# Causal attention and a max-of-three feed-forward on one core: eleven places for raw weights, low bits on GpSimd, one ring for outputs and maxima, a new plan

## The chip, the cores and the metric

The kernel runs on one core of one Trainium2 chip. A core has five instruction streams that run side by side and meet only at semaphores: TensorE (PE: matmuls, with its weight loads shown as PEld), VectorE (DVE), ScalarE (ACT), GpSimd (POOL) and SyncE (SP), which here only starts transfers. Each stream runs in the order in which it was written: an instruction that waits holds up all behind it on its engine. Matmuls write to PSUM, a small memory of banks, and DVE and ACT copy the results from there to SBUF, the core's working memory.

The metric is the device time of one launch in microseconds (us). The profile splits the same time into what each engine did.

## The reference

```python
scores = scale * np.matmul(q, k.transpose(0, 1, 3, 2))          # batch 8, heads 8, seq 576, dim 64
cum = np.cumsum(np.maximum(s, 0.0), axis=-1)
bias = -(cum[:, :, :, None] - cum[:, :, None, :])
scores = np.where(causal, -1000000000.0, scores + np.minimum(bias, 0.0))
scores = scores - np.max(scores, axis=-1, keepdims=True)
attn = np.exp(scores)
attn = attn / (np.sum(attn, axis=-1, keepdims=True) + 1e-09)
out = np.matmul(attn, v)
...
x = np.ascontiguousarray(out.transpose(0, 2, 1, 3)).reshape(B * S, H * D)   # 4608 x 512
h = np.maximum(np.maximum(x @ w1, x @ w2), x @ w3)                          # w1, w2, w3: 512 x 768
return h @ w_out                                                            # w_out: 768 x 512
```

Sixty-four heads of causal attention with a bias that decays with the distance, and then a feed-forward ("experts") whose hidden layer is the largest of three projections. All is fp32 outside.

## The kernel before

**Work.** The projections are made from pairs of 16-bit numbers: x, the weights and h are each split into a high half in fp16 and a low half that holds the rest, and each product is three fp16 matmuls (high by high, high by low, low by high). A token set is one batch in one of two phases: phase 0 has its first 256 queries, phase 1 the other 320. So there are sixteen expert sets. A set has 18 up groups (`u`, six tiles of the hidden layer by three weights, 12 matmuls each, L1479) and four down groups (`d`, 18 matmuls each, L1535).

**A set's steps.** Of three up groups of a tile the first is copied from PSUM to a buffer `m` (ACT L1490 or DVE L1494); the other two are taken into it by a scaled maximum (DVE L1502). ACT makes the high half of `h` (L1509), POOL the low one (L1514). A finished down group is scaled into an output buffer `o` by ACT (L1554) and sent by SP (L1560, `out_dram<-o`). `m` has three buffers in turn, `o` two. PSUM has three banks for `u`, `d` and whatever else goes by the name `m`.

**Set 0 is plain.** Batch 0, phase 0 is projected in fp32 straight from the raw weights (L659 to L677, down L689) while these are still being split. A raw weight is 128 x 512 numbers of 64 bits; 24 of them are loaded by SP (L477). Each goes from 64 bits to 32 by ACT (`d1`, L485), by DVE, and, from the third on, by POOL for its lowest bits (L499; the constant LOWP says which). Then a small gram product on PE (L527), its largest sum and a power of two (DVE L425 and L442, PE L434, together "power") give the scale of four weights at once; ACT makes the high half of `w` (L599), DVE the low half (L637). Raw weights lie in six places r0 to r5 and a few early buffers; each place is used again when all readers of its last weight are done.

**Attention.** It runs in units: "split" (256 queries of two head pairs of a batch), "rest" (the other 320 of one pair) and "whole" (all 576 of one pair). ORDER names them by batch: `s0` is the split units of batch 0, `r0` its rest, `w7` batch 7 whole. A unit loads q, k (`qr`) and v (`rv`) through SP, splits them (L949, L961), or for the first RAWS split units scores them in fp32 as they come. Its bias comes from running sums that DVE scans once for all heads (L375): SP spreads them to all rows from a copy in DRAM (`cd`, L880), for units 0 and 1 PE broadcasts them instead (L918). POOL lays in the causal mask (L1222). Then come the scores on PE (L1149), and the unit adds the bias and takes the row maximum on DVE (L1235), exponentials on ACT (L1244), 1/sum (L1252, L1262), splits the probabilities into two halves (ACT L1280, DVE L1288), transposes them through SP's DMAs (L1299), multiplies by v (L1384) and splits the result into x (L1429 and on).

**What sets the order.** Nothing is scheduled by the compiler: a planner in the kernel (class `Plan`) simulates the five engines. Each operation is added with the engines that may do it, a pair of durations, a key and what it reads and writes. At each moment `run` gives each free engine the ready operation with the smallest key, provided the buffers that it opens are free in the simulation; `write` then emits all in that order. For a transfer the planner keeps one clock per queue. A tag's buffers are a ring: of the kind "order" they are used in the order of creation, of the kind "free" in the order in which operations start. Constants such as PACE, EARLY, LOOK, HOLD and LATE shift keys: how far experts run behind attention, how early loads go out, how long PE keeps one tiling mode. So a constant moves instructions on every engine.

## Time and profile before

| | us |
|---|---|
| median of three timed runs | 784.83 |
| lowest and highest of the three | 783.97, 786.31 |
| the profiled execution's own time | 784.61 |
| its span in the profile | 782.6 |

| engine | busy, us | share of the span | instructions |
|---|---|---|---|
| PE | 764.8 | 98% | 7189 |
| DVE | 573.8 | 73% | 1691 |
| ACT | 519.2 | 66% | 1369 |
| POOL | 308.3 | 39% | 361 |

The profile page gives busy time by engine, the span in 40 slices (each digit the busy tenths of a slice), the DMA queues, the chain of work that ended last, and groups of instructions. A group's row reads: line, engine, operation, out<-in by the program's names, partitions x elements, count | busy us, mean ns of one | idle time of the engine just before them, and what ended most of it. The costliest groups:

```profile
L1479 PE MATMUL u<-x,w 128*128 128x320 f16 (+1 forms) x3240 | 411.3, 287 | 2.9 <-ACT o L1554 2.9
L1535 PE MATMUL d<-h,w 128*128 128x320 f16 (+1 forms) x1080 | 137.9, 287 | 0.1
L1502 DVE SCALAR_TENSOR_TENSOR m<-u,m 128x320 f32<-128x320 f32 (+1 forms) x180 | 82.2, 457 | 64.3 <-PE u L1479 60.1
```

The mean of the first row, 287 ns, is that of one form only and the row mixes two; 3240 up matmuls take 411.3 us together, and 1080 down matmuls 137.9.

A row of the timeline reads: start in us, length, engine, line, operation, tiles, count, and in brackets how long the engine had waited and for whom. A window's row reads: stretch, length, then the busy time of PE, PEld, DVE, ACT and POOL (with counts), the granted clock of PE, the share of DMA busy and GB/s.

### The profile page before, as it was taken

How to read it: one execution, taken by the hardware profiler on the slowest of the kernel's cores; microseconds unless marked ns; L12 is line 12 of the kernel's file. 1: busy time of each engine (PE TensorE's matmuls, PEld its weight loads, DVE VectorE, ACT ScalarE, POOL GpSimd, SP SyncE). 2: the span in 40 equal slices, each digit the busy share in tenths (PEclk: the TensorE clock that was granted, in tenths of full speed). 3: DMA queues.
4: the chain of work that ended last, by engine and by line, in shares of the span. 5: the costliest groups of instructions: out<-in, count | busy, mean ns of one | idle time of the engine just before them, and what ended most of it. 6: DMA issues, size and time to landing. Idle time of an engine off the chain costs nothing. (4 is left out here: it accounts for less than half of the span.)

```text
span 782.6 us, 19630 instructions
## 1 busy us (share of the span) xinstructions
PE 764.8 (98%) x7189; PEld 589.6 (75%) x7189; DVE 573.8 (73%) x1691; ACT 519.2 (66%) x1369; POOL 308.3 (39%) x361
## 2 busy tenths in 40 slices
PE   7889999999999999999999899999999999999998
PEld 5677888888888877766788677667776777778875
DVE  6999898875587888888878787888787977322131
ACT  6878777871687787986887777777876977111101
POOL 4432423641355455444544364354444452011110
PEclk9999999999999999999999999999999999999999
DMA  9799778890399899998999999898989865300000
GB/s 342 245 260 242 180 169 164 176 237 18 97 207 233 199 175 214 227 215 200 225 232 207 183 192 240 241 190 198 254 210 169 208 137 100 81 1 34 28 2 34
DMA packets 241167, 136.31 MB, mean 174 GB/s; under 512 B 204080, under 2 KB 222000, under 8 KB 241072
## 3 DMA queue, kind: packets, MB, share of 16 engines
q1 hardware_dynamic: 240912, 134.78, 75.7%
q8 instruction: 56, 0.92, 0.5%
q14 instruction: 39, 0.32, 0.2%
q10 hardware_dynamic: 160, 0.30, 0.1%
HBM read 75.64 MB, written 9.58 MB: 109 GB/s over the span
## 5 line engine op out<-in xcount | busy, mean ns | idle before, releaser
L1479 PE MATMUL u<-x,w 128*128 128x320 f16 (+1 forms) x3240 | 411.3, 287 | 2.9 <-ACT o L1554 2.9
L1479 PEld LDWEIGHTS <-w 128*128 128x128 f16 x3240 | 312.6, 98 | 99.5 <-issue 17.6
L1514 POOL TENSOR_TENSOR h<-m,h 128x320 f16<-128x320 f32 (+1 forms) x90 | 69.9, 777 | 190.4 <-ACT h L1509 174.5
L1535 PE MATMUL d<-h,w 128*128 128x320 f16 (+1 forms) x1080 | 137.9, 287 | 0.1
L1502 DVE SCALAR_TENSOR_TENSOR m<-u,m 128x320 f32<-128x320 f32 (+1 forms) x180 | 82.2, 457 | 64.3 <-PE u L1479 60.1
L1535 PEld LDWEIGHTS <-w 128*128 128x128 f16 x1080 | 104.7, 98 | 30.4 <-issue 3.2
L1222 POOL TENSOR_SCALAR_AFFINE_SELECT p<-bias 128x256 f32<-128x256 f32 (+3 forms) x91 | 68.9, 770 | 120.6 <-DVE pr L1288 68.9
L1244 ACT ACTIVATE p<-p,sc 128x256 f32<-128x256 f32 (+3 forms) x182 | 98.2, 540 | 26.3 <-DVE sc L1235 25.6
L1509 ACT ACTIVATE h<-m 128x320 f16<-128x320 f32 (+1 forms) x90 | 39.4, 438 | 102.9 <-DVE m L1502 102.6
L1288 DVE SCALAR_TENSOR_TENSOR pr<-p,sc,pr 128x256 f16<-128x256 f32 (+3 forms) x182 | 100.3, 567 | 8.0 <-ACT pr L1280 7.8
L1280 ACT ACTIVATE pr<-p,sc 128x256 f16<-128x256 f32 (+3 forms) x182 | 89.3, 538 | 13.0 <-DMA pT<-pr 7.9
L961 POOL TENSOR_TENSOR ql<-qr,qh 128x256 fp32r<-128x256 f32 (+1 forms) x76 | 82.5, 1106 | 35.0 <-ACT qh L949 30.6
L1235 DVE CUSTOM_DVE_ANT_0 p<-s,p 128x256 f32<-128x256 f32 (+3 forms) x182 | 80.4, 467 | 3.7 <-POOL p L1222 2.2
L1384 PEld LDWEIGHTS <-vv 128*64 128x64 f16 x1232 | 58.6, 110 | 18.1 <-issue 10.0
L1384 PE MATMUL av<-pT,vv 128*64 128x320 f16 (+3 forms) x1104 | 70.3, 276 | 1.2 <-DVE x L1429 0.8
L1494 DVE TENSOR_SCALAR m<-u 128x320 f32<-128x320 f32 (+1 forms) x55 | 25.3, 461 | 48.2 <-PE u L1479 47.6
L1554 ACT ACTIVATE o<-d,os 128x320 f32<-128x320 f32 (+1 forms) x60 | 28.2, 498 | 47.6 <-PE d L1535 36.8
L766 DVE TENSOR_REDUCE am<-rv 128x1 f32<-128x640 f32 (+1 forms) x44 | 33.9, 777 | 13.2 <-DMA rv<-in_qkv_dram 13.0
L1222 POOL TENSOR_SCALAR_AFFINE_SELECT ha<-bias 128x1024 f32<-128x1024 f32 (+3 forms) x29 | 26.7, 926 | 41.8 <-DVE r L1288 29.8
L1244 ACT ACTIVATE ha<-ha,sc 128x512 f32<-128x512 f32 (+3 forms) x58 | 35.9, 620 | 6.5 <-DVE sc L1235 6.1
L815 DVE SCALAR_TENSOR_TENSOR vv<-rv,vs,vv 128x640 f16<-128x640 f32 (+1 forms) x44 | 39.0, 887 | 0.4
L1288 DVE SCALAR_TENSOR_TENSOR r<-ha,sc,r 128x512 f16<-128x512 f32 (+3 forms) x58 | 37.5, 660 | 2.3 <-ACT r L1280 2.2
(170 smaller groups left out, 980.1 us busy)
## 6 DMA issues: line engine op xcount, KB each, us to landing
bias<-cd SPq DMA_DIRECT2D x32, 576.0 KB, 5.0
qr<-in_qkv_dram SPq DMA_DIRECT2D x28, 480.0 KB, 5.2
rv<-in_qkv_dram SPq DMA_DIRECT2D x32, 320.0 KB, 3.8
raw<-in_w_dram SPq DMA_DIRECT2D x16, 512.0 KB, 5.7
qr<-in_qkv_dram SPq DMA_DIRECT2D x13, 512.0 KB, 6.3
bias<-cd SPq DMA_DIRECT2D x12, 512.0 KB, 5.4
out_dram<-o SPq DMA_DIRECT2D x32, 160.0 KB, 2.4
early<-in_w_dram SPq DMA_DIRECT2D x8, 512.0 KB, 7.0
```

The lines of the kernel that those rows point to most:

```text
L961: lambda e, d0=d0, d1=d1: E[e].tensor_tensor(out=lo().bitcast(F32R)[:, d0:d1], in0=raw()[:, d0:d1], in1=hi()[:, d0:d1], op=ALU.subtract),
L1222: nc.gpsimd.affine_select(out=pt()[:, 0:8 * P].rearrange("p (j n) -> p j n", j=2)[:, :, at:at + nk], in_=r["bias"]()[:, 2 * a * w:2 * (a + ...
L1235: lambda e, j=j: nc.vector.tensor_tensor_reduce(out=pj(j), in0=src(j), in1=pj(j) if masked else bias(j), scale=-SCALE, scalar=3.0e38, op0= ...
L1244: lambda e, j=j: nc.scalar.activation(out=pj(j), in_=pj(j), func=AF.Exp, scale=-1.0, bias=nm()[:, j:j + 1], accum_out=sm()[:, j:j + 1]),
L1280: lambda e, h_=h_, s_=s_, j=j: nc.scalar.activation(out=h_(), in_=s_(), func=AF.Copy, scale=ri()[:, j:j + 1]),
L1288: lambda e, h_=h_, l_=l_, s_=s_, j=j: nc.vector.scalar_tensor_tensor(out=l_(), in0=s_(), scalar=ri()[:, j:j + 1], in1=h_(), op0=ALU.mult, ...
L1384: nc.tensor.matmul(av()[j * D:(j + 1) * D, c0:nq], lhsT=lt, rhs=rt, start=(n < 2), stop=(n >= len(todo) - 2), skip_group_check=True,)
L1479: nc.tensor.matmul(pm()[:, :nq], lhsT=v[:, wt, kt, :], rhs=x(xt, kt), start=(k == 0), stop=(k == 3 * NKT - 1),)
L1502: lambda e, pm=pm, m1=m1: nc.vector.scalar_tensor_tensor(out=m1()[:, :nq], in0=pm()[:, :nq], scalar=HSC, in1=m1()[:, :nq], op0=ALU.mult, o ...
L1509: lambda e, m1=m1, ft=ft: nc.scalar.activation(out=h(0, ft), in_=m1()[:, :nq], func=AF.Copy),
L1514: lambda e, m1=m1, ft=ft: E[e].tensor_tensor(out=h(1, ft), in0=m1()[:, :nq], in1=h(0, ft), op=ALU.subtract),
L1535: nc.tensor.matmul(pm()[:, :nq], lhsT=v[:, wt, dt, :], rhs=h(c, ft), start=(k == 0), stop=(k == 3 * NFT - 1), skip_group_check=True,)
```

## The change

It has five parts.

1. *Eleven places for raw weights* (RAWX): beside r0 to r5 and the early buffer, the two buffers each of `ql` and `qh` take raw weights as long as no split attention uses them. RAWAT says which weight lies where.
2. *Low bits on GpSimd*: LOWP covers all 24 weights, where it left out the first two.
3. *One ring for outputs and maxima*: `o` is dropped, and `m1`, the ring of the buffers `m`, has five places in place of three and holds both.
4. *The planner*: it allows eight transfers of a queue under way (LANES), keeps PE's tiling mode by looking two operations ahead (HOLD, SAME), and has other durations and rates for transfers.
5. *What runs where and when*: the masks of the first four units go to PE (MASKU, a matmul of `identb` by `tri`); the bias of unit 0 is made by four scans on DVE from rows of s, where PE broadcast it (NDB); the steps of the plain units get a key four steps ahead in place of eight (FAST); ten split units are scored in raw fp32 in place of six (RAWS); the values of two head pairs of a split unit are multiplied one behind the other (FUSE0); the low halves of `h` of the sets before the fourth go to DVE (EARLYSET); the fp16 split of the weights gets a later key (LATE); and ORDER treats batches 5 and 6 whole.

`far_power`, `split_first`, AMK, KP and MARGIN are new code that the constants leave switched off (FAR = 99, D16 = 0, KP = 0, MARGIN 0).

```diff
-PACE = (0.9, -1.0, 3000.0)
-EARLY = 8
-EARLYSET = 0
-LOOK = (10.0, 4.0, 5.0, 3.5)
+PACE = (0.5, 3.0, 3000.0)
+EARLY = 2
+EARLYSET = 4
+LOOK = (10.0, 4.0, 2.0, 3.5)
...
-MASKU = 0
+MASKU = 4
...
-FAST = 8
-HOLD = (3000.0, 30000.0)
+FAST = 4
+HOLD = (2000.0, 30000.0, 2)
+SAME = 1
...
+LANES = 8
...
+SPARE = 1000.0
...
-NDB = 0
+NDB = 1
...
-RAWS = 6
-FUSE0 = 99
+RAWS = 10
+FUSE0 = 2
...
-P3 = 10
-LOWP = (2, 24)
+P3 = 12
+RAWX = 1
+LATE = 10.0
+LOWP = (0, 24)
...
-ORDER = ('s0', 's1', 's2', 's3', 's4', 's5', 'r0', 'r1', 's6', 'r2', 'r3', 'r4', 'r5', 'r6', 'w7')
+ORDER = ('s0', 's1', 's2', 's3', 's4', 'r0', 'r1', 'r2', 'r3', 'r4', 'w5', 'w6', 'w7')
...
                     aside.append(it)
+                    if len(op.ways[e]) > 2 and len(sent) >= LANES and sent[-LANES].end > now:
+                        continue
...
-        qr=2, qh=2, ql=2, rv=4, vv=2, bias=2, p=2, pr=2, tl=2, pT0=2, pT1=2, tT=2, t=5, m1=3, o=2,
-        sc=6, dg=2, am=3, vs=5, ws=3, os=4, s=2, av=1, m=3,
+        qr=2, qh=2, ql=2, rv=4, vv=2, bias=2, p=2, pr=2, tl=2, pT0=2, pT1=2, tT=2, t=5, m1=5,
+        sc=6, far=1, dg=2, am=3, vs=5, ws=3, os=4, s=2, av=1, m=3,
...
-    def load(emit, key, nbytes, reads=(), writes=(), queue="SP", rate=0.3, lat=2000.0, begin=0.0):
-        plan.add({queue: (lat, 450.0, nbytes / rate * 1e-3)}, emit, key, reads, writes).ready = begin
+    def load(emit, key, nbytes, reads=(), writes=(), queue="SP", rate=0.36, lat=1285.0, begin=0.0, lead=1440.0):
+        plan.add({queue: (lat + SPARE, 400.0, nbytes / rate * 1e-3, lead)}, emit, key, reads, writes).ready = begin
...
+    RAWAT = [0, 1, 2, 3, 4, 5, RAW, -2, -1, -2, -1, 0, 1, 2, 3, 4, 5, -2, -1, -2, -1, 0, 1, 2]
...
             k = (i if i < RAW else i - 1) % RAW
-            if i == RAW:
+            if RAWX:
+                k = RAWAT[i]
+            if RAWX and i > RAW and k < 0:
+                r = buf("ql" if k == -1 else "qh", name=f"raw{i}")
+            elif i == RAW:
...
-            k = wkey(i)
+            k = wkey(i) + LATE
...
-            o = buf("o", free=True, name=f"o{n}_{dt}")
...
+            o = buf("m1", free=True, name=f"o{n}_{dt}")
```

How the order moves is shown at three places. In the rows, numbers behind a name tell its instances apart, and the brackets list the semaphores that the instruction waits for: `PE_49`, `DVE_49`, `Activation_49` and `Pool_49` stand for results of engines, `DMAHW0_49` to `DMAHW7_49` for eight lanes on which transfers are counted in turn.

The first place is ACT at the end of a set in the middle of the kernel, where the last two outputs of one set (`o_2`, `o_3`) stand among the attention. Before:

```order
L1252 ACTIVATE sc_7512<-sc_7512 128x2 [waits Activation_49]
L1244 ACTIVATE p_7488,sc_7519<-p_7488,sc_7519 128x512 [waits DVE_49]
L1280 ACTIVATE pr_7550<-p_7451,sc_7512 128x3x128 [waits DMAHW4_49,DMAHW3_49,DVE_49]
L1280 ACTIVATE pr_7550<-p_7451,sc_7512 128x3x128
L1244 ACTIVATE p_7488,sc_7519<-p_7488,sc_7519 128x512 [waits DVE_49]
L1252 ACTIVATE sc_7519<-sc_7519 128x2 [waits Activation_49]
L1554 ACTIVATE o_2_7574<-d_2_7493,os_5157 128x256 [waits DMAHW1_49,PE_49]
L1554 ACTIVATE o_3_7587<-d_3_7521,os_5157 128x256 [waits DMAHW2_49,PE_49]
L1490 ACTIVATE m_0_7590<-u_0_0_7553 128x320 [waits PE_49]
```

Such a place now, with all four outputs of a set:

```order
L1391 ACTIVATE pr_8708<-p_8571,sc_8663 128x3x128 [waits DMAHW3_49,DVE_49]
L1391 ACTIVATE pr_8708<-p_8571,sc_8663 128x3x128
L1593 ACTIVATE o_0_8719<-d_0_8646,os_6517 128x320 [waits PE_49]
L1593 ACTIVATE o_1_8742<-d_1_8676,os_6517 128x320 [waits PE_49]
L1593 ACTIVATE o_2_8776<-d_2_8722,os_6517 128x320 [waits PE_49]
L1355 ACTIVATE ha_8745,sc_8754<-ha_8745,sc_8754 128x512 [waits DVE_49] x2
L1363 ACTIVATE sc_8754<-sc_8754 128x2 [waits Activation_49]
L1593 ACTIVATE o_3_8807<-d_3_8756,os_6517 128x320 [waits PE_49]
```

The outputs of this set wait for PE alone, where they waited for a transfer lane too.

The second place is DVE ahead of the first down group of a regular set (`d_0`), for which all weights of the down projection and all low halves of `h` must be there. Before, the last of them was the low half of a weight, DVE's 347th instruction:

```order
L776 TENSOR_REDUCE vs_1902<-am_1373 128x1
L637 SCALAR_TENSOR_TENSOR w_1880<-early_160,rels,w_1880 128x512 [waits Activation_49]
L425 TENSOR_SCALAR vs_1902<-vs_1902 128x1 [waits DVE_49]
L637 SCALAR_TENSOR_TENSOR w_1897<-raw_1351,rels,w_1897 128x512 [waits Activation_49]
L637 SCALAR_TENSOR_TENSOR w_1905<-raw_1367,rels,w_1905 128x512 [waits Activation_49]
L442 TENSOR_REDUCE vs_1902<-m_1914 128x1 [waits PE_49]
L637 SCALAR_TENSOR_TENSOR w_1909<-raw_1473,rels,w_1909 128x512 [waits Activation_49]
L782 TENSOR_SCALAR vs_1902<-vs_1902 128x1 [waits DVE_49]
L637 SCALAR_TENSOR_TENSOR w_1912<-raw_1497,rels,w_1912 128x512 [waits Activation_49]
```

Now it is the low half of `h` itself (L1672), DVE's 414th, behind score passes (two ISA rows each, L1346) of a unit that came later before:

```order
L1346 ISA p_2096,sc_2103<-s_1941,p_2096 128x128
L1346 ISA sc_2103 128x1
L1660 SCALAR_TENSOR_TENSOR m_5_2076<-u_5_2_2080,m_5_2076 128x256 [waits DVE_49,PE_49]
L1399 SCALAR_TENSOR_TENSOR pr_2041<-p_1901,sc_1916,pr_2041 128x128 [waits DMAHW6_49,DMAHW4_49]
L1346 ISA p_2096,sc_2126<-s_1941,p_2096 128x256 [waits Pool_49]
L1346 ISA sc_2126 128x1
L1399 SCALAR_TENSOR_TENSOR pr_2041<-p_1901,sc_1916,pr_2041 128x128
L1672 TENSOR_TENSOR h_1382<-m_5_2076,h_1382 128x256 [waits Activation_49]
```

Sixty-seven more instructions of DVE stand ahead of the point at which that down group may begin.

The third place is SP at its 33rd transfer, where the twelfth to the fifteenth raw weight are now loaded in a run:

```order
L1410 DMA_TRANSPOSE pT_2_1_820<-pr_770 128x8x128 [waits DMAHW3_49,DVE_49]
L529 DMA raw_856<-in_w_dram 128x512 [waits DMAHW4_49,DVE_49]
L529 DMA raw_861<-in_w_dram 128x512 [waits DMAHW5_49,DVE_49]
L529 DMA raw_875<-in_w_dram 128x512 [waits DMAHW6_49,DVE_49]
L529 DMA raw_892<-in_w_dram 128x512 [waits DMAHW7_49,DVE_49]
L991 DMA bias_896<-cd 128x4x256 [waits DMAHW0_49,DVE_49]
```

Before, the eighth raw weight and all behind it were loaded one or two at a time, between transposes and loads of q, k and v.

## The prediction

> **What bounds the kernel now.** I read the page first: its busy shares and its 40 slices.

> ```profile
> span 782.6 us, 19630 instructions
> PE 764.8 (98%) x7189; PEld 589.6 (75%) x7189; DVE 573.8 (73%) x1691; ACT 519.2 (66%) x1369; POOL 308.3 (39%) x361
> PE   7889999999999999999999899999999999999998
> DVE  6999898875587888888878787888787977322131
> ```

> TensorE (PE) is busy 764.8 of 782.6 us. So the time is PE's own work plus 17.8 us in which it waits, and a change of order can only win from those. The windows say where they lie (columns: stretch, length, busy time of PE, PEld, DVE, ACT, POOL, then clock, DMA share, GB/s).

> ```profile
> 0.00:20.00 20.00, 16.01 (x145) 10.64 (x145) 14.03 (x58) 13.95 (x45) 9.07 (x22) 1.00 0.95 343
> 20.00:60.00 40.00, 35.59 (x362) 28.74 (x361) 38.83 (x154) 33.37 (x102) 15.92 (x22) 1.00 0.95 253
> 0.00:116.16 116.16, 105.68 (x1108) 85.52 (x1109) 103.58 (x379) 89.73 (x261) 41.52 (x69) 1.00 0.88 239
> 120.00:400.00 280.00, 280.00 (x2728) 222.95 (x2724) 220.97 (x661) 206.71 (x564) 125.69 (x144) 1.00 0.86 189
> 400.00:510.00 110.00, 106.71 (x1016) 80.58 (x1011) 90.41 (x235) 83.49 (x197) 52.76 (x55) 1.00 0.99 211
> 510.00:640.00 130.00, 129.31 (x1143) 91.62 (x1141) 108.72 (x300) 99.65 (x251) 64.11 (x66) 1.00 0.91 201
> 640.00:770.00 130.00, 130.00 (x1106) 99.21 (x1104) 48.51 (x118) 34.36 (x85) 20.51 (x25) 1.00 0.18 40
> ```

> The third row ends where the first down-projection of a regular expert set begins (L1535, 116.16 us). Up to there PE has waited 10.5 us. DVE is the other full engine of that stretch: 38.83 of 40 us in the second row. From 120 to 770 us PE waits 3.98 us in all (3.29 and 0.69); the rest of the 17.8 is the end, where the last output must be scaled and sent. The timeline of PE names the waits in the brackets.

> ```profile
> 28.19 0.23 PE L434 MATMUL m<-identb,ws 128*128 128x128 bf16 x1 [1.75 <-DVE ws L425]
> 47.16 0.23 PE L434 MATMUL m<-identb,ws 128*128 128x128 bf16 x1 [1.12 <-DVE ws L425]
> 445.49 3.42 PE L1479 MATMUL u<-x,w 128*128 128x320 f16 x24 [2.11 <-ACT o L1554]
> 499.95 0.22 PE L434 MATMUL m<-identb,vs 128*128 128x128 bf16 x1 [0.26 <-ACT o L1554]
> 500.97 3.42 PE L1479 MATMUL u<-x,w 128*128 128x320 f16 x24 [0.81 <-ACT o L1554]
> ```

> Early, PE waits for DVE. In the middle, 2.11 + 0.26 + 0.81 = 3.18 of the 3.98 us are waits for ACT's `o`, the copy of a finished down-projection out of PSUM. ACT in its turn waits for the output buffer:

> ```profile
> 440.51 0.86 SPq L1560 DMA_DIRECT2D out_dram<-o  x2
> 444.97 0.84 ACT L1554 ACTIVATE o<-d,os 128x256 f32<-128x256 f32 x2 [3.65 <-DMA out_dram<-o]
> ACT o L1554 <- DMA out_dram<-o: 8.8, 6, 3.6
> ```

> Two output buffers are in turn; the DMAs that free them were issued only at 440.51, behind other transfers on SP; ACT stood 3.65 us, the PSUM bank stayed full, and PE stood 2.11.

> **The change, part by part.** Every sum is made against the profiled execution: 784.61 us, span 782.6, so 2.0 us lie around the span. The median of three runs, 784.83, is 0.22 above it.

> *(a) PE's own work.*

> ```profile
> L1384 PE MATMUL av<-pT,vv 128*64 128x128 f16 x168 | 9.4, 219 | 0.0
> L434 PE MATMUL m<-identb,vs 128*128 128x128 bf16 x14 | 3.1, 223 | 1.2 <-DVE vs L425 1.0 <-ACT o L1554 0.3
> L918 PE MATMUL m<-early 64*128 64x256 f32 x16 | 3.8, 381 | 0.6 <-DVE early L385 0.6
> 22.26 0.93 PE L1149 MATMUL s<-qr 64*128 64x128 f32 x8
> 612.49 0.77 PE s L1149 x10
> ```

> The causal mask of the first four units moves from POOL to PE: 32 matmuls of identb by tri, 128 columns of bf16. No row shows one. From below the nearest is 9.4 / 168 = 0.056 us (64 rows of output, in a run of others), from above the lone 3.1 / 14 = 0.22; that makes 1.8 to 7.1 us, and I take 1.8, since they stand in a run like the first. Half of the bias broadcasts on PE go: 8 x 3.8 / 16 = 1.9 us less. Eight more head pairs are scored in plain fp32: 0.93 for 0.77 each at most, +0.7 at PE's pace (the next row of PE began 0.86 later, not 0.93). Two of the 14 scale broadcasts go, -0.4. Sum +0.2 us. The count of changes of tiling mode on PE is 209 for 210, so nothing comes from there.

> *(b) One ring of five buffers for outputs and maxima.* Before, an output waited for the output two earlier; now for whatever stood five places before, and four of one set's outputs can be held at once. In the order before, ACT's `o` names a DMA lane among its waits at 41 places; in the changed order at 18: two of the first set and the sixteen of the last four, behind the last attention. In the ten sets between none does. The 3.18 us of PE then lose their cause: -3.2. The wait itself moves: now it is the copy of an up-projection (`m`, 15 places of L1648 on ACT, 47 of L1652 and L1660 on DVE) that waits for the output DMA. Behind it on ACT stand exponentials and splits, on DVE the maxima that free PE's banks. What hides it: four down groups and up to three up groups of PE work lie between. Without that cover the 3.18 are back, so the term is bounded by 0 and by all of the middle waits, -3.98.

> *(c) The first 116 us.* This part is worked out from the order, and it goes against the change. Eleven places for raw weights let the loads run ahead (eleven loads before the first place is used again; SP then issues four in a row), and two weights' low bits move to POOL. But DVE gets other work. The bias of unit 0 becomes scans on DVE, and the low halves of `h` of the first sets move from POOL to DVE:

> ```profile
> L375 DVE TENSOR_TENSOR_SCAN early<-early 64x256 f32<-64x256 f32 x1 | 0.7, 676 | 0.0
> L677 DVE TENSOR_TENSOR h_plain<-u_plain,h_plain 128x256 f32<-128x256 f32 x12 | 5.0, 416 | 0.0
> L1235 DVE CUSTOM_DVE_ANT_0 p<-s,p 128x256 f32<-128x256 f32 x50 | 19.9, 415 | 0.0
> L1514 POOL TENSOR_TENSOR h<-m,h 128x256 f16<-128x256 f32 x42 | 29.8, 711 | 85.2 <-ACT h L1509 75.8 <-ACT sc L1252 9.2
> ```

> Four scans are 4 x 0.68 = 2.7 us and six low halves 6 x 0.42 = 2.5 us ahead of the first down group; twelve more score passes and their splits, standing earlier than before, are most of the rest. In the changed order 414 DVE instructions stand ahead of or at the last product which that group needs. Before, 347 did, and 379 had been executed when it began. At the mean of the third window row, 103.58 / 379 = 0.27 us, the 35 more than 379 are 9.6 us. DVE therefore needs 113.2 us of work before PE may begin the group. Its idle time in the first 20 us (5.97, waiting for s and the first scores) cannot shrink much, since unit 0 still needs both. If it never idles after that it arrives at 119.2; idling as in the second row (1.17 per 40 us, so 2.8 over 96) at 122.0. PE, with the same waits as now, would be there at 116.16 plus 2.2 us of work that now stands earlier (32 masks 1.8, two more score groups 1.7, one more value group 0.6, the eight broadcasts -1.9), so at 118.4. DVE is late by 0.8 to 3.6 us; I take 1.8, since the loads that come earlier should take some of its idling away. From below, 1.0 us less than now is possible if the first 20 us shrink by the 2 us for which the cover of filler work allows; I keep -1.0 to +3.6 for the range.

> *(d) The rest.* ACT loses some 10 us and POOL some 30 us of work (vv splits of two batches, masks, low halves). ACT is 66% and POOL 39% busy, off the path: nothing. Two batches are now treated whole instead of in two parts, which saves SP twelve transfers; the stretch at PE's end in which no attention is left only becomes longer. The tail after the last matmul, one copy and one DMA, stays. Two small attention waits (0.69 together) I leave.

> Sum: +0.2 - 3.2 + 1.8 = **-1.2 us**, 783.4 for the profiled execution and 783.6 against the median. I call it **783.5 us**: a measurement of this kernel tells a change from none from about 0.3% on, here 2.35 us, and this is less.

> **The rivals.**

> *DVE keeps up (779.5).* The loads come so early that DVE idles less than now, (c) is -1.0, and (b) takes all 3.98: 784.8 + 0.2 - 3.98 - 1.0 = 780.0. It can go lower if the new order also lets PE run nearer its best pace:

> ```profile
> L1479 PE MATMUL u<-x,w 128*128 128x256 f16 x1512 | 170.0, 273 | 0.0
> 708.66 23.58 PE u L1479 x216
> ```

> Undisturbed, 216 up matmuls take 23.58 us, 0.109 each; over the kernel they take 0.112, so 1512 of them lose 4.9 us, hidden in PE's busy time. A tenth of that is 0.5, giving 779.5. For it: loads eleven deep, and the order counts with eight transfers at a time, as SP's queue does. Against it: the DVE count above. [...]

> *DVE starves PE (791).* One mechanism: the queue of DVE ahead of the first down group. It decides from the moment that DVE idles more after 20 us than in my sum; from there each us of DVE is one of PE, and no later slack returns it. The third row less the first gives DVE's idling between 20 and 116 us as 96.16 - 89.55 = 6.6 us. If it stays so in spite of the fuller queue, DVE arrives at 125.8, PE is 7.4 late instead of 1.8, and the time is 783.5 + 5.6 = 789.1; with the masks at their upper price half way (+2) 791. For it: DVE waits in order behind results of ACT and POOL all through that stretch. [...]

> *Nothing is won in the middle.* The output wait only moves to the maxima: 783.5 + 3.2 = 786.7, no change. The same would be seen if the shared ring did not do what it says. For it: SP's queue, behind which the output DMAs stand, is as full as before.

> **How the numbers follow.** The forecast with its own spread (781.3 to 785.5) gets 0.42, of which 0.08 lies below 782.5 and 0.34 within 0.3%. DVE keeping up gets 0.30, all of it faster. DVE starving PE gets 0.20, slower. Nothing won in the middle gets 0.08: 0.05 within, 0.03 slower. So faster 0.38, no difference 0.39, slower 0.23. The range for 8 in 10 reaches from 777.5 (the first rival with another 2 us of PE's pace) to 789.5 (most of the second).

> **What would show it.** (a) PE busy within 2 us of 764.8. (b) No wait of an up matmul for ACT's `o` near the ends of sets, and no `o` waiting for out_dram; in its place DMA waits at `m`. (c) PE idle before its first down group between 10 and 14 us, DVE busy over 95% from 20 to 120 us. I am wrong if DVE's busy share there is below 93% while PE waits, if PE's busy time moves by over 3 us, or if a new wait of over 1 us recurs after 120 us.

## The result, and the profile after

| us | before | after |
|---|---|---|
| median of three runs | 784.83 | 797.75 |
| lowest and highest | 783.97, 786.31 | 796.06, 798.24 |
| profiled execution | 784.61 | 798.24 |
| its span | 782.6 | 796.3 |

The changed kernel is slower: ratio 1.0138, 95% interval 1.0100 to 1.0177. The forecast was 783.5 and its range ended at 789.5, so the time lies 8.3 us outside. The two spans differ by 13.7 us. The page of the changed kernel, in the same lines as before, with PE's granted clock in the last:

```profile
span 796.3 us, 19549 instructions
PE 775.0 (97%) x7195; PEld 591.4 (74%) x7195; DVE 573.2 (72%) x1696; ACT 510.5 (64%) x1355; POOL 272.1 (34%) x314
PE   6999999999999989999899999999999999999998
DVE  5999999888577697797877887886987873122121
PEclk8999999999999999999989999999999999999999
```

PE is busy 10.2 us longer (775.0 for 764.8) and waits 3.5 us longer (21.3 for 17.8). Two slices show a clock under 0.9, the first and the twenty-first; before, the clock was 1.00 in every stretch shown. That is the profiled execution: over all executions timed here and beside the runs below, the mean granted clock was 0.993 to 1.000 for the kernel before, and 0.989 to 0.994 for the changed one. The windows, in the columns used above:

```profile
0.00:123.35 123.35, 114.59 (x1156) 88.75 (x1157) 109.42 (x402) 88.00 (x259) 26.84 (x47) 0.96 0.82 237
20.00:120.00 100.00, 98.08 (x1064) 78.17 (x1064) 95.22 (x355) 79.31 (x232) 21.36 (x32) 0.99 0.80 220
240.00:400.00 160.00, 151.61 (x1369) 108.11 (x1367) 129.69 (x325) 120.07 (x286) 74.65 (x77) 0.99 0.95 207
400.00:640.00 240.00, 239.09 (x2239) 174.85 (x2233) 197.17 (x583) 191.60 (x516) 111.48 (x121) 0.99 0.86 185
```

And three of them before:

```profile
20.00:120.00 100.00, 93.51 (x1007) 78.20 (x1005) 91.13 (x328) 78.58 (x226) 35.32 (x50) 1.00 0.86 213
240.00:400.00 160.00, 160.00 (x1526) 119.98 (x1525) 133.27 (x365) 126.44 (x322) 75.76 (x82) 1.00 0.97 216
400.00:640.00 240.00, 236.01 (x2157) 172.20 (x2152) 199.13 (x534) 183.13 (x447) 116.87 (x120) 1.00 0.94 206
```

PE waits less up to its first down group of a regular set, now at 123.35 us for 116.16 (8.76 for 10.48), and, in this execution, from 400 us on (0.91 for 3.99). From 240 to 400 us, where it never waited before, it now waits 8.39. PE's timeline names the waits, two at the start and three in the middle:

```profile
11.59 0.49 PE L1260 MATMUL s<-qr 64*128 64x128 f32 x4 [1.49 <-issue]
17.64 2.93 PE L1435 MATMUL m<-pr-4_281,p-4_242 128*128 128x128 f32 x12 [3.75 <-POOL pr-4_281 L1425]
288.52 0.23 PE L458 MATMUL m<-identb,vs 128*128 128x128 bf16 x1 [1.58 <-DVE vs L449]
341.51 0.23 PE L458 MATMUL m<-identb,vs 128*128 128x128 bf16 x1 [1.02 <-DVE vs L449]
399.32 0.29 PE L458 MATMUL m<-identb,vs 128*128 128x128 bf16 x1 [3.89 <-DMA bias<-cd]
```

The three in the middle are one kind: the power step of a batch's v, in which PE broadcasts the largest value of v over all rows. They make 6.49 of the 8.39 us.

**Followed back, the longest.** The last of the three is put down to `bias`, but the row of v itself was late. The rows of SP and DVE ahead of it:

```profile
373.86 7.87 SPq L1410 DMA_TRANSPOSE pT<-pr  x2
381.82 3.46 SPq L1218 DMA_TRANSPOSE pT<-r  x2
385.38 3.16 SPq L1227 DMA_TRANSPOSE tT<-tl  x2
388.63 0.53 SPq L861 DMA_DIRECT2D rv<-in_qkv_dram  x1
389.25 1.61 SPq L1410 DMA_TRANSPOSE pT<-pr  x1
390.92 0.83 SPq L861 DMA_DIRECT2D rv<-in_qkv_dram  x1
395.64 0.82 DVE L874 TENSOR_REDUCE am<-rv 128x1 f32<-128x640 f32 x1 [1.06 <-DMA rv<-in_qkv_dram]
399.12 0.15 DVE L449 TENSOR_SCALAR vs<-vs 128x1 bf16<-128x1 f32 x1
```

The last load of v is issued at 390.92, its maximum comes from 395.64 on, the broadcast can start at 399.3, and PE has stood still. In the planner's own simulation of this order the last load of v stands at 372.4 and the broadcast at 382.65. The load is 18.5 us later than planned and the broadcast 16.7, while PE's other work runs some 13 us late there (the table below). The load itself was not slow: DVE began on it 4.7 us after its issue, and the plan allows 5.6. Its issue was late. SP started the pair of transposes at 373.86 and reached that load 17.1 us later, one issue behind the other; in the plan the same nine transfers follow each other from 362.2 to 372.4, in 10.2 us. The plan left the transfers less slack than they needed.

**Followed back, the first.** ACT at the start of the changed kernel:

```profile
9.28 0.60 ACT L1037 ACTIVATE bias<-m 128x512 f32<-128x512 f32 x1 [6.48 <-PE m L1029]
14.69 0.48 ACTq L425 DMA_DIRECT2D cd<-early  x1
15.22 0.40 ACT L1355 ACTIVATE p-4_242<-p-4_242,sc 128x128 f32<-128x128 f32 x1 [5.34 <-DMA raw<-in_w_dram]
```

The transfer `cd` before:

```profile
7.60 0.48 ACTq L401 DMA_DIRECT2D cd<-early  x1
```

The transfer that sends the running sums to DRAM (`cd`) is issued by ACT, and its place in ACT's order is now ahead of the first exponentials. Beside DVE it waits for the landing of a raw weight's load, which the bracket names; both are counted on one transfer lane. ACT was idle for 5.34 us, up to 15.22, with `cd` issued only at 14.69. The exponentials, the row sums and PE's matmuls stood behind it: the 3.75 us above.

**The clock.** Fine windows at the edges of the two stretches at a lower clock, with the clock as the third number from the end:

```profile
11.50:12.00 0.50, 0.41 (x4) 0.33 (x4) 0.50 (x3) 0.00 (x0) 0.00 (x0) 1.00 1.02 410
12.00:12.50 0.50, 0.50 (x6) 0.29 (x4) 0.50 (x2) 0.00 (x0) 0.38 (x1) 0.50 1.01 401
22.00:22.50 0.50, 0.50 (x4) 0.06 (x2) 0.50 (x4) 0.50 (x4) 0.00 (x0) 0.76 1.07 373
397.50:398.00 0.50, 0.00 (x0) 0.00 (x0) 0.50 (x3) 0.50 (x3) 0.00 (x0) 0.71 1.27 276
404.50:405.00 0.50, 0.50 (x14) 0.44 (x12) 0.00 (x0) 0.00 (x0) 0.50 (x2) 0.96 1.05 67
```

From 12.0 to 22.24 and from 397.71 to 404.54 us the granted clock was 0.50, just behind and within the long waits: 10.24 and 6.83 us.

### The profile page after: what moved, and what is told of

Its sections match the earlier page's. It is cut to its first block, busy times and chain, and to the rows that moved or that the text cites. A ratio compares the mean times of both kernels' runs of the same rounds, so it can differ in the third digit from the quotient of the medians.

```text
span 796.3 us, 19549 instructions
## 1 busy us (share of the span) xinstructions
PE 775.0 (97%) x7195; PEld 591.4 (74%) x7195; DVE 573.2 (72%) x1696; ACT 510.5 (64%) x1355; POOL 272.1 (34%) x314
## 4 chain that ended last, share of the span: by engine, by line
PE 74%; DMA 9%; DVE 8%; ACT 5%; issue 3%; SPq 0%; POOL 0%; ACTq 0%; DVEq 0%; POOLq 0%
PE u L1637 39%; PE d L1574 15%; PE av L1495 7%; PE s L1260 6%; DMA rv<-in_qkv_dram 3%; PE u_plain L753 3%; PE s L1141 2%; DMA qr<-in_qkv_dram 2%; PE d_plain L797 1%; DMA raw<-in_w_dram 1%; DVE pr L1399 1%; ACT p L1355 1%; DMA pT<-pr 1%; DMA pT<-r 1%; DVE ha L1346 1%
## 5 line engine op out<-in xcount | busy, mean ns | idle before, releaser
L1660 DVE SCALAR_TENSOR_TENSOR m<-u,m 128x320 f32<-128x320 f32 (+1 forms) x180 | 82.1, 456 | 65.1 <-PE u L1637 60.4
L1672 POOL TENSOR_TENSOR h<-m,h 128x320 f16<-128x320 f32 (+1 forms) x72 | 56.1, 780 | 182.0 <-ACT h L1667 176.2
L1355 ACT ACTIVATE p<-p,sc 128x128 f32<-128x128 f32 (+3 forms) x192 | 104.0, 543 | 22.3 <-DVE sc L1346 22.1
L1399 DVE SCALAR_TENSOR_TENSOR pr<-p,sc,pr 128x128 f16<-128x128 f32 (+3 forms) x184 | 104.7, 582 | 9.1 <-ACT pr L1391 8.9
L1391 ACT ACTIVATE pr<-p,sc 128x128 f16<-128x128 f32 (+3 forms) x184 | 91.5, 546 | 23.5 <-DVE sc L1373 13.7
L1072 POOL TENSOR_TENSOR ql<-qr,qh 128x256 fp32r<-128x256 f32 (+1 forms) x64 | 70.8, 1126 | 39.0 <-ACT qh L1060 35.1
L1346 DVE CUSTOM_DVE_ANT_0 p<-s,p 128x512 f32<-128x512 f32 (+3 forms) x168 | 77.8, 489 | 2.8 <-POOL p L1333 2.5
L1495 PEld LDWEIGHTS <-vv 128*64 128x64 f16 x1232 | 59.9, 112 | 18.4 <-issue 7.5
L1495 PE MATMUL av<-pT,vv 128*64 128x320 f16 (+3 forms) x1104 | 71.6, 281 | 1.3 <-DVE x L1540 0.6
L1652 DVE TENSOR_SCALAR m<-u 128x256 f32<-128x256 f32 (+1 forms) x61 | 27.7, 454 | 55.5 <-PE u L1637 55.1
L1333 POOL TENSOR_SCALAR_AFFINE_SELECT ha<-bias 128x768 f32<-128x768 f32 (+3 forms) x28 | 23.3, 840 | 45.7 <-DVE r L1399 28.1
L1399 DVE SCALAR_TENSOR_TENSOR r<-ha,sc,r 128x384 f16<-128x384 f32 (+3 forms) x56 | 35.7, 646 | 4.3 <-ACT r L1391 4.1
L1391 ACT ACTIVATE r<-ha,sc 128x384 f16<-128x384 f32 (+3 forms) x56 | 30.6, 596 | 12.4 <-DMA pT<-r 6.4
```

Of the source, the lines that this page charges most:

```text
L1072: lambda e, d0=d0, d1=d1: E[e].tensor_tensor(out=lo().bitcast(F32R)[:, d0:d1], in0=raw()[:, d0:d1], in1=hi()[:, d0:d1], op=ALU.subtract),
L1333: nc.gpsimd.affine_select(out=pt()[:, 0:8 * P].rearrange("p (j n) -> p j n", j=2)[:, :, at:at + nk], in_=r["bias"]()[:, 2 * a * w:2 * (a + ...
L1346: lambda e, j=j: nc.vector.tensor_tensor_reduce(out=pj(j), in0=src(j), in1=pj(j) if masked else bias(j), scale=-SCALE, scalar=3.0e38, op0= ...
L1355: lambda e, j=j: nc.scalar.activation(out=pj(j), in_=pj(j), func=AF.Exp, scale=-1.0, bias=nm()[:, j:j + 1], accum_out=sm()[:, j:j + 1]),
L1391: lambda e, h_=h_, s_=s_, j=j: nc.scalar.activation(out=h_(), in_=s_(), func=AF.Copy, scale=ri()[:, j:j + 1]),
L1399: lambda e, h_=h_, l_=l_, s_=s_, j=j: nc.vector.scalar_tensor_tensor(out=l_(), in0=s_(), scalar=ri()[:, j:j + 1], in1=h_(), op0=ALU.mult, ...
```

## A second view: how far the chip lags behind the plan

The kernel's planner writes down when it expects each operation. The table gives, at eleven times of the plan, the start of an up group on the chip less the start that the planner gave it (us; e1 to r16 are the experiments below, r5 is the changed kernel again). A flat row is a plan that the chip keeps to; a rising one loses time there.

```
plan time     80  130  200  250  300  350  400  450  500  570  750   plan's end
before       0.5  0.6  0.5  0.6  0.1 -0.1 -0.2  2.0  3.0  2.8  3.9   778.4
after        8.5  7.7  7.1  7.2 10.6 12.6 19.1 19.4 19.9 20.9 20.9   775.6
e1           5.0  4.3  4.6  4.7  7.5 10.8 16.8 16.8 17.3 18.0 18.0
e4           7.8  7.0  6.4  6.5  8.9 10.7 14.1 17.7 19.6 22.3 22.3
r9           5.8  6.3  6.2  5.3  5.3  6.4  7.0  7.0  7.0  7.0  7.4   778.7
r11          0.5 -1.6 -1.6 -1.6 -1.8  1.8  5.5  5.8  6.5  6.8  6.5   786.2
r13          4.2  3.6  3.8  3.9  3.9  3.8  4.8  4.8  4.8  4.8  5.5   778.4
r15          4.8  4.2  4.1  4.1  6.1  8.4  9.6 10.2 10.3 10.0  9.8   778.8
r16          9.2  9.7 12.3 12.8 18.0 18.2 20.1 21.1 26.2 26.4 26.5   776.2
```

The new plan is only 2.8 us shorter than the old one (775.6 for 778.4), and the chip is 17.0 us further behind it at the end. It loses 8 us before plan time 80 and 13.7 from 250 to 570.

## The experiments

Times are medians; the ratio is to the kernel before, run on the same chip in the same set.

**e1 to e3: the two waits that stand out.** In e1 the `cd` transfer, in e2 the power step of v on PE is put later in the order that is written out; e3 does both. `delay` writes what it names, and what depends on it, n operations of that engine later.

```diff
# e1
+    seq = delay(seq, lambda op: op.eng == "ACT" and len(op.ways["ACT"]) > 2 and any(b.tag == "cd" for b in op.bufs), "ACT", 10)
# e2
+    seq = delay(seq, lambda op: op.eng == "PE" and op.start > 150.0e3 and any(b.tag in ("vs",) for b in op.bufs), "PE", 2)
```

> Edit: of the changed kernel only one step moves. The transfer that sends the running sums to DRAM (cd, issued by ACT) stands ten ACT operations later, behind the first exponentials; nothing else is planned anew. Theory A (ACT stood 5.3 us at that issue because its transfer lane was still taken, PE stood 3.75 us behind ACT, and the clock fell to half after it): ACT's exponentials start near 10.5 us instead of 15.2, PE's wait of 3.75 falls under 1.5, the granted clock stays at 1.0 in the first 25 us; 797.75 - 3 to 3.75 - 3 = 791 to 792 us. Rival B (VectorE bounds the first 116 us, so PE only waits later): the wait returns before 120 us and the time stays within 1 us of 797.75.

> Edit: of the changed kernel only the small matmuls that broadcast the row maximum of v (L458 on vs, after 150 us of the plan), with what hangs on them, stand two PE operations later. Theory A (these matmuls hold up PE's queue while DVE waits for v's transfer): the three waits of 1.58, 1.02 and 3.89 us go, the clock does not fall at 397.7 us (about 2.5 us at half clock saved): 797.75 - 6.5 - 2.5 = 789 us. Rival B (the transfers of v are late for everything, so the wait moves to the products with v, L1495, or to scores): 795 to 798 us, with new waits of PE of 1 us and more between 270 and 420 us.

> Edit: both moves together. If both theories hold and the two places are independent: 797.75 - 6.5 - 9 = 782 to 783 us, under the kernel before (784.83); PE busy about 769, clock 1.0 throughout. If either wait comes back elsewhere, the sum of the two single gains is not reached.

Measured: e1 796.6, ratio 1.0124 [1.0100, 1.0148]; e2 797.29, 1.0133 [1.0101, 1.0165]; e3 794.14, 1.0097 [1.0075, 1.0119]. In e1 the start does what was meant (ACT's and PE's timeline):

```profile
10.28 0.40 ACT L1355 ACTIVATE p-4_242<-p-4_242,sc 128x128 f32<-128x128 f32 x1 [0.24 <-DVE sc L1346]
13.97 2.93 PE L1435 MATMUL m<-pr-4_279,p-4_242 128*128 128x128 f32 x12 [0.95 <-POOL pr-4_279 L1425]
397.76 0.23 PE L458 MATMUL m<-identb,vs 128*128 128x128 bf16 x1 [4.18 <-DVE vs L449]
```

The exponentials begin at 10.28 for 15.22, PE's wait falls from 3.75 to 0.95, and the 3 us won at the start are kept to the end of that profile (lag 18.0 for 20.9). The clock fell all the same, to 0.50 from 12.34 to 19.17 us, and the middle is untouched. The 791 to 792 us expected did not come: 1.0124 is within the interval of the changed kernel, so the time shows no clear gain. In e2 the wait at the broadcast is gone, but it comes back elsewhere (PE's timeline):

```profile
292.96 1.66 PE L1495 MATMUL av<-pT,vv 128*64 128x320 f16 x24 [1.18 <-DVE m L1660]
555.62 0.69 PE L1495 MATMUL av<-pT,vv 128*64 128x256 f16 x12 [1.86 <-DMA pT<-pr]
```

So e2 went by its rival B. PE's order by itself is not the cause: put the broadcast later, and a later operation waits, for a maximum `m` on DVE or for a transfer. e3 gained some 3 us where 15 were expected.

**e4: is it the clock?** Idle PE time in the first units is filled with 31 extra matmuls (2.1 us by the groups). They change the values of one score tile.

```diff
+    def fill(n):
+        ps = sp().rearrange("p (a n) -> p a n", a=2)
+        for k in range(n):
+            c["nc"].tensor.matmul(
+                ps[:, 0, o + qb * 128:o + qb * 128 + 128], lhsT=c["identb"](), rhs=c["tri"](), start=False, stop=True,
...
+        if op is ones[-1]:
+            fill(9)
+        if op is at[2]:
+            fill(22)
```

> Edit: nothing is moved or removed; PE is given 31 extra matmuls (the mask of one early score tile added again, which leaves its masked places masked) in its two waits of the start, 9 at 10.1 us and 22 at 13.9 us. Theory A (idle time of PE lowers the clock, and the lower clock is a cost of its own beside the wait): PE's clock stays at 1.0 in the first 25 us though ACT is as late as before; about 3 us less, 794.5 to 795.5 us. Rival B (the clock falls for another reason, such as the kind of matmul or the time since the start): the clock still falls, and the time is the same or up to 1 us longer.

Measured: 798.6, ratio 1.0142 [1.0114, 1.0169]. The page of e4:

```profile
PE 772.4 (97%) x7226; PEld 589.9 (74%) x7226; DVE 571.3 (72%) x1696; ACT 509.8 (64%) x1355; POOL 271.9 (34%) x314
```

The filler's group:

```profile
L1756 PE MATMUL s-2_217<-tri,identb 128*128 128x128 bf16 x31 | 2.1, 219 | 0.0
```

The clock was 1.000 over the whole span of the profiled execution (0.994 to 0.998 over the other three). PE was busy 772.4 - 2.1 = 770.3 without the filler, 4.7 less than after: about what the low clock adds to busy time, as far as two executions can be compared. But the kernel was no faster, and the execution at full clock was the slowest of the four. PE came sooner and waited longer (25.3 us in all for 21.3; the lag reaches 22.3). So the clock is not what sets the end: where it is mended, PE waits for its inputs instead, at v's broadcast above all (9.6 us in the group of L458 on `vs`).

**r5 and r6: the causal masks on PE.** r5 is the changed kernel once more, r6 leaves the mask matmuls of the first four units out.

```diff
-                        stop=(masked and n == len(terms) - 1), skip_group_check=True,
+                        stop=(n == len(terms) - 1), skip_group_check=True,
...
-                if not masked:
+                if False:
```

> The changed kernel itself once more, as the mark for the other runs of this set: 1.0138 of the kernel before by the first measurement, so some 11 us over it. If the low clock (two stretches of 10.2 and 6.8 us in its first profile) and the waits for v at 288, 341 and 399 us are the same in every execution, they are found again at the same places.

> Edit: the changed kernel in its own order without the 32 mask matmuls (L1271): the causal mask of the first four units is left out. Theory A (PE's own work grew by 5.6 us, of which the masks and the score groups that they cut in two are 3.3 and up to 2.9, and PE bounds the kernel): 5 to 6 us less than the changed kernel in this set, PE busy 5 us less. Rival B (the masks lie in time in which PE waits for ACT anyway, at 10 to 18 us): 0 to 1 us less.

Measured: r5 799.89, ratio 1.0154 [1.0123, 1.0185], with the same waits up to 400 us and the same two stretches at half clock (0.989 over the span, as in the first profile); r6 794.3, 1.0089 [1.0060, 1.0119], 5.6 us less than r5, as theory A had it. One thing is not the same in r5. From 400 to 640 us PE waited 3.69 us, where the first profile had 0.91:

```profile
400.00:640.00 240.00, 236.31 (x2216) 172.92 (x2213) 195.72 (x572) 189.39 (x507) 111.15 (x120) 0.99 0.88 184
```

The scores in the changed kernel:

```profile
L1260 PE MATMUL s<-qr 64*128 64x256 f32 x72 | 12.3, 420 | 0.0
```

What follows the scores of unit 0 on PE's timeline, in the changed kernel:

```profile
8.11 1.56 PE L1029 MATMUL m<-early 64*128 64x256 f32 x6
```

The same in r6:

```profile
6.64 1.89 PE L1029 MATMUL m<-early 64*128 64x256 f32 x8
```

The scores in r6:

```profile
L1260 PE MATMUL s<-qr 64*128 64x256 f32 x72 | 10.8, 377 | 0.0
```

With eight masks among them the scores of unit 0, two head pairs, run from 5.13 to 8.11 us, in r6 from 5.13 to 6.64. That is 1.47 us for 8 masks, 0.18 each and 5.9 for 32, close to the upper bound of the prediction (0.22). This holds what the masks cost the scores around them, 420 ns for 377, though part of the 420 is the half clock (394 in e4). The same matmul in e4's run of 31 fillers takes 2.1 / 31 = 0.068 us. The planner, too, reckons with the price of a run: it adds 144 ns for two masks, 2.3 us for 32. A mask (128*128) stands between scores (64*128) and costs 0.18 us there for 0.068 in a run of its own kind; what makes the difference no run shows.

**r7 and r8: the shared ring alone.** r7 is the changed order with the old rings (`m1` of 3, `o` of 2), r8 is the old order with the shared ring.

```diff
# r7, in the changed kernel
-        pools[tag] = ctx.enter_context(tc.tile_pool(name=f"k{tag}", bufs=depth[tag]))
+        pools[tag] = ctx.enter_context(tc.tile_pool(name=f"k{tag}", bufs=3 if tag == "m1" else depth.get(tag, 2)))
...
# r8, in the kernel before
-        pools[tag] = ctx.enter_context(tc.tile_pool(name=f"k{tag}", bufs=depth[tag]))
+        pools[tag] = ctx.enter_context(tc.tile_pool(name=f"k{tag}", bufs=5 if tag == "m1" else depth[tag])) if tag != "o" else None
...
```

The planner goes on counting with the rings of its kernel, so each order stays as it was.

> Edit: the changed kernel in its own order, but the buffers are three for maxima and two for outputs, as before. Theory A (the shared ring took away the 3.2 us of PE's waits for outputs): these waits come back, 2 to 4 us more than the changed kernel. Rival B (the new order alone keeps outputs apart, or the wait is hidden): within 1 us of it.

> Edit: the kernel before in its own order, with one ring of five for maxima and outputs and nothing else of the change. Theory A: the waits of 2.11, 0.26 and 0.81 us for outputs go: 3 us less than before, ratio 0.996. Rival B (the wait moves to the maxima, or what stands behind takes it): within 1 us of before.

Measured: r7 804.67, ratio 1.0242 [1.0195, 1.0290], 4.8 us more than r5 (its six executions spread from 801.79 to 811.05); r8 785.45, 0.9984 [0.9960, 1.0008]. From the list of waits (who waits <- for whom: us in all, times, longest), in r7:

```profile
PE u L1637 <- ACT o L1593: 2.6, 3, 1.6
ACT o L1593 <- DMA out_dram<-o: 26.9, 10, 4.7
```

The same waiter in the changed kernel:

```profile
ACT o L1593 <- PE d L1574: 40.8, 26, 3.5
```

The ring does its work: without it ACT stands 26.9 us for output transfers, with it none. In the old order the gain of 3.2 us that the prediction counted is not there: the point estimate is 1.2 and no difference is within the interval. The `o` waits were gone in r8's profile, but smaller waits stood in their place, for `m`, `h`, v's maximum and a transpose, none over 0.77 us. From 400 to 640 us PE waits as long in it as before, 3.95 us for 3.99:

```profile
400.00:640.00 240.00, 236.05 (x2167) 172.01 (x2164) 198.94 (x529) 182.90 (x445) 117.01 (x120) 1.00 0.96 209
```

Its clock was 0.50 for 3.4 us at 28.6.

**r9 to r12: the planner's numbers.** r9 gives the changed kernel the old durations and rates of all transfers, no limit of eight, and e1's later `cd` (the lines below are some of its places); r10 also puts the masks back on POOL (MASKU 0). r11 does the reverse: the kernel before with the new transfer numbers and the limit. r12 is r8 with the power step one operation later on PE.

```diff
-LANES = 8
+LANES = 999
...
-    def load(emit, key, nbytes, reads=(), writes=(), queue="SP", rate=0.36, lat=1285.0, begin=0.0, lead=1440.0):
-        plan.add({queue: (lat + SPARE, 400.0, nbytes / rate * 1e-3, lead)}, emit, key, reads, writes).ready = begin
+    def load(emit, key, nbytes, reads=(), writes=(), queue="SP", rate=0.3, lat=2000.0, begin=0.0, lead=450.0):
+        plan.add({queue: (lat, 450.0, nbytes / rate * 1e-3, lead)}, emit, key, reads, writes).ready = begin
...
-                {"SP": (1570.0 + SPARE, 1250.0, 1250.0, 545.0)},
+                {"SP": (2000.0, 1250.0, 1600.0, 1250.0)},
```

> Edit: the changed kernel planned anew with the planner's costs of before for transfers (longer latencies, 0.3 in place of 0.36 of rate, no limit of eight), and cd's transfer ten ACT operations later as in e1. The plan itself then ends at 778.7 us in place of 775.6. Theory A (the middle is lost because the plan believes that transfers are faster than they are, so that PE's broadcasts of v's maximum stand too early): PE's lag behind the plan grows by at most 3 us between 248 and 570 us, where it grew by 13.7, and the time is 778.7 + 5 + 3 + some 2 = 787 to 790 us. Rival B (the middle is lost to the denser attention, whatever the costs say): the lag grows by 10 us and more, 795 us and over.

> Edit: as r9_old_costs, and the masks of the first four units stay on POOL (MASKU 0). The plan ends at 778.1 us. Theory A: PE's own work is 766 to 768 us as before, PE's lag is 2 to 4 us at 100 us and 3 to 5 at the end: 782 to 785 us, about as fast as the kernel before or a little faster. Rival B (other parts of the change cost too): over 788 us.

> Edit: the kernel before planned anew with the changed planner's costs for transfers and its limit of eight under way, nothing else of the change. The plan ends at 786.2 us in place of 778.4. Theory A (the new costs are too low for the middle): PE's lag behind the plan, which was within 0.7 us up to 440 us, grows to 5 us and more, and the time is 791 us or more. Rival B (the new costs are right or too high, and the lag has another cause): the lag stays under 3 us and the time is 787 to 790 us, only as much slower as the plan says.

> Edit: the kernel before in its own order with one ring of five, and the matmuls that broadcast a maximum (L434 on ws and vs, after 20 us) one PE operation later. Theory A (these matmuls hold up PE 4.7 us in the profile of before, and one operation later their input is there): 0.9984 of the ring alone less 3 to 4 us: 781 to 783 us, under both kernels. Rival B (what they feed, the weights' splits on DVE, is late then and PE waits for it): 785 us and more.

Measured: r9 787.91, ratio 1.0020 [1.0002, 1.0038]; r10 787.42, 1.0019 [0.9995, 1.0043]; r11 794.14, 1.0094 [1.0068, 1.0121]; r12 785.69, 1.0009 [0.9985, 1.0033]. The middle window of r9:

```profile
240.00:400.00 160.00, 158.44 (x1466) 114.02 (x1463) 135.09 (x341) 123.88 (x292) 78.67 (x81) 1.00 0.97 219
```

The broadcast of v in r9 that stood at 399.32 after:

```profile
395.46 0.23 PE L458 MATMUL m<-identb,vs 128*128 128x128 bf16 x1 [0.45 <-DMA bias<-cd]
```

The middle window of r11:

```profile
240.00:400.00 160.00, 154.48 (x1447) 115.94 (x1445) 130.97 (x363) 121.45 (x311) 74.48 (x81) 0.99 0.90 202
```

With the old numbers PE waits 1.56 us in the middle for 8.39, and the ratio falls by a full point from e1's, 1.0124 to 1.0020: some 8 us. The "longer latencies" of r9's expectation do not fit its edit. With SPARE the changed planner reckons 4.6 us from issue to landing for one load of v (320 KB), the old one 3.5, and the median measured in the changed kernel is 3.9. For a load, only the rate at which a full queue is worked off is the more hopeful one in the changed kernel.

The kernel before loses 0.9% with the new numbers alone. Its time alone does not decide between the two theories: its plan is 7.8 us longer (786.2 for 778.4), and 785.82 + 7.8 is 793.6, so the 787 to 790 us named for rival B were too low. The place decides. Run again, the longer plan has its idle time of PE at the start (8.1 us up to 116 us where the old plan has 2.6, but only 0.3 from 240 to 400). On the chip PE waits 5.52 us from 240 to 400 us, where the kernel before waits for nothing, and the lag grows by 8.4 us from plan time 250 to 570, where that of the kernel before grows by 2.2.

r12 missed its 781 to 783: its 785.69 went by its rival B. r10 missed its 782 to 785. Its masks are off PE (767.4 busy), but PE waits at the start instead:

```profile
13.60 1.65 PE L1260 MATMUL s<-qr 64*128 64x128 f32 x8 [5.53 <-DVE sc L1346]
```

and the clock was at half for 13.7 us from 11.2 on.

**r13 and r14: the start, and ORDER.** r13 is r10 with the start of before (NDB 0, FAST 8) and a longer hold of `cd`; r14 is r13 with the old ORDER.

```diff
-FAST = 4
+FAST = 8
...
-NDB = 1
+NDB = 0
```

> Edit: the changed kernel with the planner's old costs for transfers, masks on POOL, the bias of unit 0 by PE's broadcast and the keys of the first units as before (NDB 0, FAST 8), and cd's transfer sixteen ACT operations later. Left of the change: eleven raw places, low bits on POOL for all weights, the shared ring, RAWS, EARLYSET, LATE, PACE and the order of units. The plan ends at 778.4 us, as that of before. Theory A (r10's remaining loss is its start): no wait over 2 us and no low clock in the first 25 us, lag behind the plan 1 to 3 us at 100 us and 4 at the end: 780 to 784 us, ratio 0.993 to 0.998. Rival B (the rest of the change costs something by itself): 786 us or more.

> Edit: as r13_old_start, with the order of units of before (s5, s6, r5 and r6 in place of w5 and w6). The plan ends at 779.8 us. If the new order of units is worth something by itself, this is 1 to 3 us slower than r13; if not, the same within 1 us.

Measured: r13 785.88, ratio 0.9987 [0.9974, 1.0000]; r14 787.66, 1.0020 [1.0005, 1.0036]. r13 and r8 (0.9984) are the best versions of the study, each about 1 us under the kernel before, which is at the edge of what can be measured; r13's expectation was 0.993 to 0.998. One wait remains at its start, followed by 3.4 us of half clock:

```profile
22.81 1.34 PE L1495 MATMUL av<-pT,rv 128*64 128x256 f32 x8 [4.35 <-ACT pT L1445]
```

Between r13 and r14 lies the new ORDER, with batches 5 and 6 whole: worth about 0.3%.

**r15 and r16: rates, or what a transfer costs its queue?** Both are the changed kernel with e1's `cd`. r15 takes back only the rates of loads and transposes (those of outputs and bias stay new), r16 only the lead times.

```diff
# r15, with the other transposes at 200.0 a block for 156.0
-    def load(emit, key, nbytes, reads=(), writes=(), queue="SP", rate=0.36, lat=1285.0, begin=0.0, lead=1440.0):
+    def load(emit, key, nbytes, reads=(), writes=(), queue="SP", rate=0.3, lat=1285.0, begin=0.0, lead=1440.0):
...
-                {"SP": (1570.0 + SPARE, 1250.0, 1250.0, 545.0)},
+                {"SP": (1570.0 + SPARE, 1250.0, 1600.0, 545.0)},
...
# r16, with the other transposes, the bias and the outputs in the same way
-    def load(emit, key, nbytes, reads=(), writes=(), queue="SP", rate=0.36, lat=1285.0, begin=0.0, lead=1440.0):
+    def load(emit, key, nbytes, reads=(), writes=(), queue="SP", rate=0.36, lat=1285.0, begin=0.0, lead=450.0):
...
-                {"SP": (1570.0 + SPARE, 1250.0, 1250.0, 545.0)},
+                {"SP": (1570.0 + SPARE, 1250.0, 1250.0, 1250.0)},
```

> Edit: the changed kernel planned anew with only the rates of its transfers as before (0.3 in place of 0.36 for loads, 200 in place of 156 ns a block of a transpose, 1600 in place of 1250 for the tall ones); the limit of eight, the latencies and the leads stay new; cd's transfer ten ACT operations later. The plan ends at 778.8 us. Theory A (the new rates are too high; the middle is limited by what the DMA queues carry): the lag behind the plan grows by at most 3 us between 250 and 570 us, and the time is as r9, 1.002 of before, 786 to 789 us. Rival B (the leads or the limit of eight do it): the lag grows by 8 us and more, 793 us or over.

> Edit: the changed kernel planned anew with only the leads as before (450 ns for loads, 1250 for transposes, from the start of an issue to the moment from which its bytes count); rates, latencies and the limit of eight stay new; cd's transfer ten ACT operations later. The plan ends at 776.2 us. Theory A: the lag grows by 8 us and more between 250 and 570 us, as in the changed kernel, 793 us or over. Rival B: it grows by at most 3 us, 785 to 789 us.

Measured: r15 788.92, ratio 1.0023 [1.0007, 1.0040]; r16 799.81, 1.0146 [1.0115, 1.0176]. The middle window of r15:

```profile
240.00:400.00 160.00, 154.98 (x1399) 110.63 (x1395) 131.44 (x323) 120.08 (x289) 74.49 (x77) 1.00 0.96 207
```

Of r16:

```profile
240.00:400.00 160.00, 155.35 (x1395) 109.92 (x1393) 132.57 (x331) 120.93 (x284) 75.59 (x77) 0.99 0.97 214
```

The rates alone bring r9's time back; the lead times bring nothing. So the rates are the part that costs. Not all of it is explained. The lag of r15 still grows by 5.9 us from 250 to 570, where r9's grows by 1.7 and r16's by 13.6. PE's waits in this one window do not part the two runs either (5.0 us in r15, 4.7 in r16). DMA is as busy in all of them (0.95 to 0.97, 207 to 219 GB/s).

The planner's own books fit that share only at the old rates. Run again, it fills the queue from 240 to 400 us of its clock with 155.5 us of transfers in r9 and 155.7 in r15, but with 132.5 in the changed kernel and in r16, for about as many transfers (101, 99, 102 and 102). A measured share of 0.95 is 152 of these 160 us. So at the new rates the plan sees room that is not there. How the lateness divides between full DMA engines and SP, which issues in order and stood at its transposes (one pair took 7.87 us in the rows above), was not tried apart.

## Why the prediction was wrong, step by step

- *The frame* (PE's work plus its waits, nothing else) held: 10.2 + 3.5 = 13.7. It took for granted that the clock stays at 1.0. The clock fell in two stretches that follow new waits, which is about 4.7 of the 10.2 by e4; that these waits cause it is argued from their order in time.
- *(a) PE's own work, +0.2:* mis-sized. Without the clock PE's work grew by 5.5 (770.3 for 764.8). The term that failed is the 32 masks at 0.056 us, from a run of matmuls of one kind; between scores they cost 0.18, 5.9 in all for 1.8, and the upper bound of 7.1 was the nearer row. With the other terms of (a), -1.6, that makes 4.3 of the 5.5; 1.2 stays unexplained. "The count of changes of tiling mode is 209 for 210, so nothing comes from there" misled: each mask stands among scores of another shape, as the lone row of the upper bound did among other work.
- *(b) The ring, -3.2:* half right. No `o` waits for output transfers any more, and in the new order the old rings cost 4.8 us (r7). But the 3.2 us were not won. From 400 to 640 us PE waited 0.91 us in the first profile of the changed kernel, but 3.69 in r5, the same kernel, and 3.95 in r8, the ring alone, for 3.99 before: other waits stood in the place of those for `o`. That is the rival "Nothing is won in the middle", though not through the maxima alone (0.76 us of r8's waits are for `m`).
- *(c) The first 116 us, +1.8 from a full DVE:* wrong in its mechanism. DVE was as full as said, 95.2% from 20 to 120 us, but PE waited there less than before, 1.92 us for 6.49. The first down group of a regular set began at 123.35 us for 116.16, and not for longer waits: PE had waited 8.76 us for 10.48, but its own work up to there took 114.59 us for 105.68. The masks (5.9 by r6) and the half clock until 22.2 (some 3.2, an estimate: half of the 6.5 us in which PE was busy then) make up these 8.9 us. Of the two long waits at the start, 5.24 us (1.49 + 3.75), a later `cd` took 3.3 in e1. The order showed that transfer as ACT's sixth row, and I counted only DVE's rows: the step counted instructions on one engine where it had to look for waits that stand in front of an engine's queue.
- *(d) The rest, nothing:* the step that failed most. "The planner has other durations and rates for transfers" was part of the change, and it was costed through the order alone. The new order asks for v sooner than SP and the DMA queues bring it; 8.4 us of waits from 240 to 400 us are the result, plus the half clock from 397.7 on. r9 and r15 win a full point of the ratio back, some 8 us, and r16 wins nothing: the rates do it.
- *The rival "DVE starves PE", 791:* the right sign through the wrong engine. The waits that it priced between 20 and 116 us shrank. No rival had the transfers of the middle late, so the range could not reach the time. Of the three signs of being wrong that the prediction names, two came: PE's busy time moved by 10.2 us, and new waits of over 1 us recur after 120 us. The order was compared by counts of instructions and never by asking whether a planned time still holds when the times that the plan assumes are wrong.

## What to carry to other kernels

Where a kernel's order is planned from a table of costs, a change of these costs is a change of every slack in the program: compare the plan's own clock with the trace, and the transfer time that it books in a stretch (here 132.5 of 160 us) with the measured share of DMA (0.95). Here times per byte that were cut by 17 to 22% showed as 8.39 us of waits, most of them at one kind of operation with no slack, far from any edited line. A transfer issued by a compute engine is an instruction that can block it, as `cd` did ACT for 5.34 us; look for it in the order ahead of the first work. And a small matmul put among matmuls of another shape, 0.18 us a mask here, was priced better by the lone row of the trace (0.22) than by the row of a run (0.056).
